# Moving loads, weight splits and a softplus in an attention-and-MLP kernel

## The chip, the cores and the metric

The kernel runs on one core of a Trainium2 chip. The time is the device time of one execution in microseconds (us); lower is better.

## The reference

```python
kv  = einsum('bhsd,bhse->bhde', k, v)          # b, h, s, d = 8, 8, 576, 64
out = einsum('bhsd,bhde->bhse', q, kv)
x   = out / sqrt(mean(out*out, -1) + 1e-6) * g_norm   # laid out as 4608 tokens x 512
h   = x @ w_in                                  # 512 x 2048
g   = h * erf(softplus(h))
y   = g @ w_out                                 # 2048 x 512
```

Everything is float32 (the weights come as float64 and are converted on the chip). Most products are done in a faster float32 form of TensorE (FP32R in the code), for which each operand is split into an upper form, a lower form and a combination of both; three products of these forms replace one exact product. In the trace of the kernel before, the same piece of `h` took 2.7 us in this form (264.02 to 266.74) and 3.4 us exact (146.09 to 149.53).

## The kernel before

The tokens go in nine blocks of 512. Blocks 0 and 1 take the weights as they arrive. While block 1 runs, in sixteen steps, the kernel also splits every weight column block into its three parts and stores the parts (786 KB each) to memory. From the third block on, parts are fetched back in a stream, in periods of four steps. This document calls block 1 "the second block" and what follows "the streamed blocks". Beside this, the attention of the next block is done a piece at a time.

In the profiles PE is TensorE (matmuls), ACT is ScalarE, DVE is VectorE, and SP issues most transfers. Results of TensorE land in banks of the PSUM memory; a bank can be written again when ScalarE or VectorE has copied it out. The copies named below are the *bank copy* (`h_sb`, ScalarE), the *qT copy* (the transposed q, ScalarE) and `bd_kv` (the k-v products, VectorE); the *squares' halves* (`sq_hi`, `sq_lo`) are VectorE's split of the attention's squares.

The loads of k, v and q of one head pair, two pairs ahead:

```python
    def load_pair(i):
        T, p = divmod(i, NP)
        ...
        t = q_sb[T, p] = pool.tile([P, J, 2, D], FP32, name="q_sb", tag="q")
        nc.sync.dma_start(out=t, in_=q[...].rearrange("h (p j) d -> p j h d", j=J))
        for name, got, src in (("k", k_sb, k), ("v", v_sb, v)):
            C = chunks(T)                       # 6 in block 0, else 5
            rows, rest = divmod(S, C)           # 96 and 0, else 115 and 1
            t = got[T, p] = pool.tile([rows + rest, 2, C, D], FP32, ...)
            side.dma_start(out=t[:rows]..., in_=heads[:, : S - rest]...)
            if rest:
                side.dma_start(out=t[rows:, :, 0], in_=heads[:, S - rest :]...)
```

The split of a weight block. The upper form is made by ScalarE in one step, the other two by VectorE at the start of the next, and then the store is issued. `w_new` has four buffers, so a step's uppers need the stores of two steps before to have landed:

```python
    def upper_w(x, high):
        nc.scalar.activation(high, x, AF.Copy, scale=(1.0 + 2.0**-13) / SHIFT)

    def lower_w(x, high, low, both):
        nc.vector.scalar_tensor_tensor(out=low, in0=high, scalar=SHIFT, in1=x, ...)
        nc.vector.tensor_tensor(out=both, in0=high, in1=low, op=ALU.subtract)
```

One step of blocks 0 and 1 (cuts marked with `...`):

```python
    for n in range(FIRST * FC + 1):
        T, f = divmod(n, FC)
        ...
            for key in list(w_new)[:2]:
                w_lower(*key)
            for piece in steps[f][0]:           # halves, norm, split of the attention
                piece()
        ...
            n_ps, m_ps = hidden(T, f, turns=False)
        ...
                nc.scalar.activation(h, n_ps, AF.Copy, scale=SHIFT - 1.0)
                add(h, m_ps)                    # VectorE
            nc.scalar.activation(s, h, AF.Softplus)
            if T == FIRST - 1:
                ...
                gates(done)
                for key in list(w_new):
                    w_lower(*key)
                for key in to_cut[f]:
                    w_upper(*key)
            for piece in steps[f][1]:           # apply, mean
                piece()
            if f % BATCH == BATCH - 1:
                ...                             # four erfs, with two table loads
        if n >= LAG:
            project(f2, hs[n - LAG], last)
        ...
            for piece in steps[f][2]:           # k, v products and q transposes
                piece()
```

And the end of a streamed period, where parts are fetched and finished results are stored:

```python
        for j in range(J):
            result(T2, b2, j, g, w)
            fetch(BATCH + j)                    # the last one fetches two w_out parts
            if b2 == NB - 1:
                store(T2, j, es.pop(j))
```

At the boundary from the second block to the streamed ones, the result tile of block 1 and a tile `h` that the second streamed period fills share a buffer: `h` waits until the last of four result stores has landed.

Of the kernel before, what the change touches and what calls it, by code (L numbers as in the profile page):

```python
# [43 lines left out]
AF = mybir.ActivationFunctionType  # L44
# [11 lines left out]
WHOLE = 2  # L56
# [4 lines left out]
def kernel(  # L61
# [10 lines left out]
    nc = tc.nc  # L72
    P = 128
    B, H, S, D = q.shape
# [6 lines left out]
    FC = DF // P  # L81
# [180 lines left out]

    xT, x_forms, tails = {}, {}, {}

    def attention(T, p, pools=None):

        st = {}

        halves = FIRST <= T < B
# [14 lines left out]
        def products():  # L284

            kv_ps = st["kv"] = bank("kv_ps")
            ks, vs, qs = (x.pop((T, p)) for x in (k_sb, v_sb, q_sb))
            C = chunks(T)
            for c in range(C):
                rows = slice(0, S // C + (c < S % C))  # L290
                for i in range(2):
                    s = slice(i * D, i * D + D)
                    nc.tensor.matmul(  # L293
                        kv_ps[s, s],
                        lhsT=ks[rows, i, c],
                        rhs=vs[rows, i, c],
                        start=(c == 0),
                        stop=(c == C - 1),
                    )
            if p % 2 == 0:  # L300
                nc.tensor.transpose(kv_ps[:, q_tail], q_last[:, p // 2], ident)
            if p == NP - 2:
                for i in range(NP):
                    load_last(T + 1, i)
            st["qT"] = square_tile("qT")
            for i in range(2):
                s = slice(i * D, i * D + D)
                nc.vector.tensor_copy(out=bd[s, s], in_=kv_ps[s, s])
            if p % 2 == 0:
                tails[T] = attp.tile([P, P], FP32, name="qT_last", tag="t")  # L310
                nc.vector.tensor_copy(out=tails[T], in_=kv_ps[:, q_tail])
            st["tail"] = tails[T][:, p % 2 * R : p % 2 * R + R]
            qt_ps = bank("qt_ps")
            for j in range(J):
                nc.tensor.transpose(qt_ps[:, j * P : j * P + P], qs[:, j], ident)  # L315
            nc.scalar.copy(st["qT"], qt_ps)
# [67 lines left out]
            if T >= FIRST:  # L384
                thirds(st.pop("x"), *(form[:, p] for form in x_forms[T]))

        def products_and_loads():
            products()
            load_pair(T * NP + p + 2)

        if T == 0:
            return products, apply, halve, mean, norm
        first = (products_and_loads, apply) if T < B else (lambda: None, square)
        return (*first, halve if halves else lambda: None, mean, norm, split)


    def upper(x, high):
# [163 lines left out]
    first = [attention(0, p, banks_0 | {"se_ps": (ps_o, f"o{p}")}) for p in range(NP)]  # L561
# [51 lines left out]

    others = [("in", f) for f in range(WHOLE)]
    others += [("out", f) for f in (*range(FC - BATCH, FC), *range(FC - BATCH))]
    places_w = {4: 0, 5: 1, 8: 0, 9: 1, FC - 4: 0, FC - 3: 1}
    to_cut = {f: [] for f in range(FC)}
    for f in range(FC):
        if f < FC - BATCH:
            to_cut[f] = [("in", f + WHOLE), others.pop(0)]  # L620
        elif f == FC - BATCH:
            to_cut[f] = [("in", FC - 2), ("in", FC - 1)]
        if f in places_w:
            to_cut[f].append((*others.pop(0), places_w[f]))
# [13 lines left out]
    for n in range(FIRST * FC + 1):  # L638
        T, f = divmod(n, FC)
        if n == FC:  # L640
            early_room.close()
            late = ctx.enter_context(tc.tile_pool(name="late", bufs=1))
            x_new = ctx.enter_context(tc.tile_pool(name="x_new", bufs=1))
            acc = ctx.enter_context(tc.tile_pool(name="acc", bufs=1))
            w_in_p = ctx.enter_context(tc.tile_pool(name="w_in_p", bufs=BATCH))
            low = low_room.enter_context(tc.tile_pool(name="low", bufs=1))
            forms = late.tile([P, 3, KC, G], FP32R, name="x_forms0")
            x_forms[FIRST] = [forms[:, i] for i in range(3)]
        if T < FIRST:
            if f == 0:  # L650
                steps = pieces_of(T + 1)
            if due(1):
                weights()
            for key in list(w_new)[:2]:
                w_lower(*key)
            for piece in steps[f][0]:
                piece()
        while due(0):
            weights()
        done = n - LAG + 1  # L660
        if T == 0 and done >= 0:
            gates(done)
        if T == FIRST - 1:
            if f == 0:
                x_high = wide.tile([P, KC, G], FP32R, name="x_high", tag="h")
                x_low = low.tile([P, KC, G], FP32R, name="x_low")
                for i in range(0, KC, 2):
                    upper(xT[T][:, i : i + 2], x_high[:, i : i + 2])
                for i in range(0, KC, 2):
                    lower_only(xT[T][:, i : i + 2], x_high[:, i : i + 2], x_low[:, i : i + 2])  # L670
        if T == FIRST - 1 and f >= WHOLE:
            n_ps, m_ps = hidden(T, f, turns=False)
        elif T < FIRST:

            if n > 1:
                plain[n] = ps_h.tile([P, G], FP32, name="h_ps", tag="h")
                blocks = [(n, c) for c in range(KC)]
            elif n == 0:
                for i, (pool, tag) in enumerate(((ps_at, "at"), (ps_o, "o0"))):
                    plain[i] = pool.tile([P, G], FP32, name="h_ps", tag=tag)  # L680
                blocks = [(i, c) for c in range(KC - 1) for i in range(2)] + [(0, KC - 1)]
            else:
                blocks = [(1, KC - 1)]
            for i, c in blocks:
                nc.tensor.matmul(  # L685
                    plain[i],
                    lhsT=w_in_sb[:, c, i % FC * P : i % FC * P + P],
                    rhs=xT[T][:, c, :],
                    start=(c == 0),
                    stop=(c == KC - 1),  # L690
                )
        if T < FIRST:
            if n == whole:
                old_h = acc.tile([P, BATCH, G], FP32, name="h", tag="e")
            h = hs[n] = old_h[:, n - whole] if n >= whole else unit("h_sb")
            s = ss[n] = unit("s_sb")
            if n in plain:
                nc.scalar.copy(h, plain.pop(n))
            else:
                nc.scalar.activation(h, n_ps, AF.Copy, scale=SHIFT - 1.0)  # L700
                add(h, m_ps)
            nc.scalar.activation(s, h, AF.Softplus)
            if T == FIRST - 1:
                if f == 1:
                    x_both = wide.tile([P, KC, G], FP32R, name="x_both", tag="h")
                    for i in range(0, KC, 2):
                        both_only(x_high[:, i : i + 2], x_low[:, i : i + 2], x_both[:, i : i + 2])
                    x_forms[T] = x_high, x_low, x_both
                gates(done)
                for key in list(w_new):  # L710
                    w_lower(*key)
                for key in to_cut[f]:
                    w_upper(*key)
            if n == 0:
                w_next("split")
            for piece in steps[f][1]:
                piece()
            if f % BATCH == BATCH - 1:
                for i in range(n - BATCH + 1, n + 1):
                    nc.scalar.activation(ss[i], ss[i], AF.Erf)  # L720
                softplus_table()
            if T == FIRST - 1:
                load_parts("in", {FC - 3: 2, FC - 2: 1, FC - 1: 1}.get(f, 0))
        if n >= LAG:
            T2, f2 = divmod(n - LAG, FC)
            last = n - LAG in (FC - 1, whole - 1)
            project(f2, hs[n - LAG], last)
            if last:
                sums(*((acc, "e") if T2 < FIRST - 1 else (wide, "h")))
                if T2 == 0:  # L730
                    for j in range(J):
                        store(T2, j, es.pop(j))
        if T < FIRST:
            for piece in steps[f][2]:
                piece()
# [44 lines left out]
    for m in range(first_batch, batches + 1):  # L780
        T, b = divmod(m, NB)
# [8 lines left out]
        def piece():  # L790
            if todo:
                todo.pop(0)()
# [22 lines left out]
        if m < batches:  # L815
            h = wide.tile([P, BATCH, G], FP32, name="h", tag="h")
            s = gate_r.tile([P, BATCH, G], FP32, name="s", tag="s")
# [70 lines left out]
```

## Time and profile before

| before | |
|---|---|
| median of the first runs | 960.7 us |
| span of the profiled execution | 958.2 us |
| TensorE busy | 931.0 us, 97% |
| TensorE idle in the second block | 4.15 us, in six waits |
| wait of TensorE at the boundary | 4.10 us |

The page gives the busy time of each engine and, in 40 slices, its busy tenths. The waits say who waited for whom; the timeline shows each instruction with the idle time before it in brackets; the chain of waits goes back from an instruction to what released it. The prediction shows the lines that carry it. One line more of ScalarE's timeline belongs to them (start, us, source line, operation, idle before it and what ended it):

```profile
189.89 0.63 ACT L423 ACTIVATE w_new<-w_in_sb 128x512 fp32r<-128x512 f32 x1 [2.26 <-DMA w_in<-w_new]
191.69 0.64 ACT L423 ACTIVATE w_new<-w_out_sb 128x512 fp32r<-128x512 f32 x1 [1.16 <-DMA w_out<-w_new]
```

At these two lines ScalarE stands still for 3.4 us in all, because two stores have not landed.

### The profile page before, as it was taken

What the parts mean: (1) busy time and instruction counts of PE and PEld (TensorE: products, weight loads), DVE (VectorE), ACT (ScalarE), POOL (GpSimd) and SP (SyncE); (2) the same over time, 40 slices, a digit from 0 to 9 for tenths busy, and PEclk for the clock granted to TensorE, in tenths of its full rate; (3) what the DMA queues carried; (4) which work ended last, traced back from release to release, by engine and by line L of the source; (5) the groups of instructions that cost most, each with busy time, mean ns of one, the idle gap of its engine ahead of it and who ended that gap; (6) DMA issues with size and microseconds to landing.
All of it is one profiled execution on the core that took longest, in us unless ns stands there. A gap on an engine that the chain in (4) does not pass through costs nothing.

```text
span 958.2 us, 11752 instructions
## 1 busy us (share of the span) xinstructions
PE 931.0 (97%) x4272; PEld 684.5 (71%) x4272; DVE 741.0 (77%) x1054; ACT 616.5 (64%) x825; POOL 2.4 (0%) x10
## 2 busy tenths in 40 slices
PE   6999999989998999999999999999999999999998
PEld 4444445556576788888888888888888788878886
DVE  3979957777675788888888888878788877778667
ACT  3889875577663666666666666666666666665552
POOL 0000000000000000000000000000000000000000
PEclk9999999999999999999999999999999999999999
DMA  9857505688899887899888978988897779768872
GB/s 257 284 163 212 159 1 234 253 315 292 287 326 328 322 301 262 249 319 335 305 255 318 331 286 281 317 321 287 271 340 263 263 249 353 274 257 298 337 274 66
DMA packets 111842, 259.78 MB, mean 271 GB/s; under 512 B 43864, under 2 KB 69544, under 8 KB 111784
## 3 DMA queue, kind: packets, MB, share of 16 engines
q1 hardware_dynamic: 110152, 256.73, 76.4%
q10 hardware_dynamic: 1568, 2.29, 0.8%
q8 instruction: 34, 0.56, 0.2%
q14 instruction: 24, 0.20, 0.1%
q0 software_dynamic: 64, 0.00, 0.0%
HBM read 224.40 MB, written 34.60 MB: 270 GB/s over the span
## 4 chain that ended last, share of the span: by engine, by line
PE 78%; ACT 8%; DVE 8%; DMA 4%; issue 1%; SPq 0%; DVEq 0%; ACTq 0%
PE n_ps L456 41%; PE m_ps L456 21%; PE o_ps L514 5%; PE h_ps L685 3%; PE se_ps L321 2%; PE kv_ps L293 2%; PE qt_ps L315 1%; DMA v_sb<-in_v_dram 1%; DMA out_dram<-e 1%; DMA w_out<-w_new 1%; ACT L103 1%; DVE h L848 1%; ACT w_e L215 1%; ACT s_sb L720 1%; DVE h L439 1%
## 5 line engine op out<-in xcount | busy, mean ns | idle before, releaser
L456 PE MATMUL n_ps<-x_forms,w_in_parts 128*128 128x512 f32 x896 | 234.7, 404 | 5.7 <-ACT h L828 4.1
L456 PE MATMUL n_ps<-w_out_parts,g_forms 128*128 128x512 f32 x928 | 231.5, 391 | 0.0
L456 PEld LDWEIGHTS n_ps<-x_forms,w_in_parts 128*128 128x128 f32 x896 | 167.3, 189 | 50.1 <-issue 9.1
L456 PEld LDWEIGHTS n_ps<-w_out_parts,g_forms 128*128 128x128 f32 x928 | 174.1, 188 | 38.7 <-issue 1.7
L830 ACT ACTIVATE s<-h 128x512 f32<-128x512 f32 x112 | 71.0, 634 | 180.4 <-DVE h L439 180.4
L439 DVE TENSOR_TENSOR h<-m_ps,h 128x512 f32<-128x512 f32 x116 | 79.8, 688 | 65.6 <-ACT h L828 50.7
L456 PE MATMUL m_ps<-w_out_parts,g_forms 128*128 128x512 f32 x464 | 124.2, 389 | 0.0
L456 PE MATMUL m_ps<-x_forms,w_in_parts 128*128 128x512 f32 x448 | 120.3, 390 | 0.0
L514 PE MATMUL o_ps<-w_out_sb,h_sb 128*128 128x512 f32 x224 | 100.8, 592 | 0.3 <-DVE h_sb L636 0.3
L456 PEld LDWEIGHTS m_ps<-w_out_parts,g_forms 128*128 128x128 f32 x464 | 87.1, 188 | 18.1
L456 PEld LDWEIGHTS m_ps<-x_forms,w_in_parts 128*128 128x128 f32 x448 | 84.5, 189 | 17.9
L439 DVE TENSOR_TENSOR e<-m_ps,e 128x512 f32<-128x512 f32 x116 | 80.3, 692 | 17.6 <-PE m_ps L456 10.5
L434 DVE SCALAR_TENSOR_TENSOR e<-n_ps,e 128x512 f32<-128x512 f32 x88 | 60.3, 686 | 38.0 <-PE n_ps L456 38.0
L514 PEld LDWEIGHTS o_ps<-w_out_sb,h_sb 128*128 128x128 f32 x224 | 42.3, 190 | 48.9 <-issue 46.6
L828 ACT ACTIVATE h<-n_ps 128x512 f32<-128x512 f32 x112 | 65.6, 586 | 14.1 <-DMA out_dram<-e 10.2
L405 DVE SCALAR_TENSOR_TENSOR g_forms<-g_forms 128x1024 fp32r<-128x1024 f32 x58 | 71.1, 1226 | 2.0
L402 DVE TENSOR_TENSOR g_forms<-h,g_forms 128x1024 fp32r<-128x1024 f32 x58 | 70.6, 1218 | 1.7 <-ACT g_forms L399 1.4
L399 ACT ACTIVATE g_forms<-h 128x1024 fp32r<-128x1024 f32 x58 | 58.9, 1060 | 12.5 <-PE m_ps L456 9.8
L848 DVE TENSOR_TENSOR h<-h,s 128x1024 f32<-128x1024 f32 x56 | 66.0, 1219 | 0.7 <-ACT s L834 0.7
L685 PE MATMUL h_ps<-xT,w_in_sb 128*128 128x512 f32 x144 | 64.9, 594 | 0.8 <-DVE w_in_sb L240 0.6
L106 ACT ACT_TABLE_LOAD x44 | 56.5, 1283 | 0.7
L834 ACT ACTIVATE s<-s 128x1024 f32<-128x1024 f32 x56 | 56.2, 1052 | 0.3
(98 smaller groups left out, 1014.9 us busy)
## 6 DMA issues: line engine op xcount, KB each, us to landing
w_out_parts<-w_out SPq DMA_DIRECT2D x116, 768.0 KB
w_in_parts<-w_in SPq DMA_DIRECT2D x112, 768.0 KB
w_in<-w_new SPq DMA_DIRECT2D x16, 768.0 KB
q_sb<-in_q_dram SPq DMA_DIRECT2D x32, 256.0 KB
w_raw<-in_moe_w_out_dram SPq DMA_DIRECT2D x8, 1024.0 KB
out_dram<-e SPq DMA_DIRECT2D x32, 256.0 KB
k_sb<-in_k_dram SPq DMA_DIRECT2D x28, 287.5 KB
v_sb<-in_v_dram SPq DMA_DIRECT2D x28, 287.5 KB
```

Of the source, the lines that this page charges most:

```text
L106: nc.scalar.preload_act_table_set("softplus")
L399: nc.scalar.activation(high, x, AF.Copy, scale=1.0 + 2.0**-13)
L402: nc.vector.tensor_tensor(out=low, in0=x, in1=high.bitcast(FP32), op=ALU.subtract)
L405: nc.vector.scalar_tensor_tensor(out=both, in0=low.bitcast(FP32), scalar=SHIFT, in1=high.bitcast(FP32), op0=ALU.mult, op1=ALU.add,)
L434: nc.vector.scalar_tensor_tensor(out=out_, in0=ps, scalar=scale, in1=out_, op0=ALU.mult, op1=ALU.add)
L439: nc.vector.tensor_tensor(out=out_, in0=ps, in1=out_, op=ALU.add)
L456: nc.tensor.matmul(ps, lhsT=weights(form, k), rhs=moving(form, k), start=(form == forms[0] and k == 0), stop=(form == forms[-1] and k == 3),)
L514: nc.tensor.matmul(o_ps[j], lhsT=g[:, j * P : j * P + P], rhs=w_out_sb[:, f, :], start=(f == 0), stop=last,)
L685: nc.tensor.matmul(plain[i], lhsT=w_in_sb[:, c, i % FC * P : i % FC * P + P], rhs=xT[T][:, c, :], start=(c == 0), stop=(c == KC - 1),)
L828: nc.scalar.activation(h[:, i], n_ps, AF.Copy, scale=SHIFT - 1.0)
L830: nc.scalar.activation(s[:, i], h[:, i], AF.Softplus)
L848: nc.vector.tensor_tensor(out=part(h, half), in0=part(h, half), in1=part(s, half), op=ALU.mult)
```

## The change

The intent is to let the weight parts through first, to spread the stores, and to use ScalarE's wait for VectorE. Three parts, called A, B and C below. A, the loads:

```diff
-        def products_and_loads():
-            products()
+        def loads():
             load_pair(T * NP + p + 2)
 ...
-        first = (products_and_loads, apply) if T < B else (lambda: None, square)
-        return (*first, halve if halves else lambda: None, mean, norm, split)
+        if T == B:
+            return lambda: None, square, lambda: None, mean, norm, split
+
+        pieces = ((products,), (apply,), (halve, loads)) if halves else ((products, loads), (apply,), ())
+        return (*(partial(chain, *group) for group in pieces), mean, norm, split)
```

B, the list of splits, with w_out ahead of w_in and the six extras elsewhere:

```diff
-    places_w = {4: 0, 5: 1, 8: 0, 9: 1, FC - 4: 0, FC - 3: 1}
+    places_w = {3: 0, 5: 1, 6: 0, 8: 1, 9: 2, 10: 0}
 ...
-            to_cut[f] = [("in", f + WHOLE), others.pop(0)]
+            to_cut[f] = [others.pop(0), ("in", f + WHOLE)]
```

C, the uppers ahead of the softplus:

```diff
-            nc.scalar.activation(s, h, AF.Softplus)
             if T == FIRST - 1:
 ...
                 for key in to_cut[f]:
                     w_upper(*key)
+            nc.scalar.activation(s, h, AF.Softplus)
```

More of the change, by code (lines that the diff above doesn't have):

```diff
@@ L263, with chain @@
     xT, x_forms, tails = {}, {}, {}
+    def chain(*pieces):
+        for piece in pieces:
+            piece()
     def attention(T, p, pools=None):
```

## The prediction

> **What bounds the kernel now.** I read the page's busy shares first, then the waits of TensorE, then its timeline at each wait, then what the waits lead back to. The page:
>
> ```profile
> span 958.2 us, 11752 instructions
> PE 931.0 (97%) x4272; PEld 684.5 (71%) x4272; DVE 741.0 (77%) x1054; ACT 616.5 (64%) x825; POOL 2.4 (0%) x10
> PE   6999999989998999999999999999999999999998
> PEclk9999999999999999999999999999999999999999
> ```
>
> TensorE is busy for 931.0 of 958.2 us, so all its idle time is 27.2 us, 2.8% of the span. The change leaves TensorE's own instructions and their order alone (the comparison of the two kernels' instruction orders has no difference on TensorE; only ScalarE, VectorE and the DMA queue are reordered). It can win only idle time, and what a slowed clock costs after it. The stretch table says where: 2.3 us idle in 20 to 40 us, 1.8 in 60 to 100 (both before anything that the change moves), 4.2 in 160 to 260, 4.6 in 280 to 320, 1.6 in 760 to 860, the rest at the start and at the end. From 320 to 760 TensorE is never idle. So I ask what it waits for in 140 to 320 us (columns: us in total, times, longest):
>
> ```profile
> PE n_ps L456 <- ACT h L828: 4.1, 1, 4.1
> PE se_ps L321 <- ACT qT L316: 2.0, 2, 1.0
> PE n_ps L456 <- ACT h_sb L700: 1.7, 2, 1.0
> ```
>
> The last two, with 0.46 of small ones, are the second token block (148 to 262 us), where the weights are split into parts and stored: idle of 1.02 at 178, 0.20 at 186, 1.03 at 197, 0.65 at 206, 0.99 at 210 and 0.26 at 256 us, 4.15 in all. In the chain of waits, the piece at 197 leads back like this (start, us, what):
>
> ```profile
> 182.68 8.98 DMA w_out<-w_new
> ...
> 191.69 0.64 ACT w_new L423
> ...
> 192.34 1.28 ACT L103
> ...
> 196.96 0.61 ACT h_sb L700
> ...
> 197.61 2.13 PE n_ps L456 x8
> ```
>
> A store of finished parts takes 8.98 us to land, ScalarE waits for its buffer, then does the norm with two table loads, and copies a PSUM bank out too late. The first wait is the boundary to the streamed blocks, here in stretches of 4 us (PE, PEld, DVE, ACT, POOL busy, clock, DMA share, GB/s):
>
> ```profile
> 292.00:296.00 4.00, 3.62 (x14) 2.30 (x13) 0.00 (x0) 0.00 (x0) 0.00 (x0) 1.00 1.02 389
> 296.00:300.00 4.00, 0.29 (x1) 0.29 (x2) 0.30 (x1) 0.60 (x1) 0.00 (x0) 1.00 0.39 128
> 300.00:304.00 4.00, 4.00 (x12) 3.09 (x12) 3.48 (x5) 1.70 (x4) 0.00 (x0) 0.57 1.02 266
> ```
>
> All engines stand; the chain puts 9.86 us here on the last store of a result (issued at 289.06), whose tile the next h needs. After it the clock is 0.57 for 4 us: 4 x 0.43 = 1.7 us more are lost. The boundary costs 4.1 + 1.7 = 5.8 us.
>
> **What the Trainium skill says.** "DMA: Bandwidth & Descriptors", section "Why a DMA increments its semaphore by 16 and not by 1": a copy from these queues runs on k engines, the largest k up to 16 that divides both sides' slowest dimension, the lowest-numbered ones. k and v come as 115 rows: k = 5. The trace agrees: in 296 to 300 us, where only the queue's remainder runs, the share is 0.39, near 5/16 = 0.31, and in 260 to 264 it is 0.32. So k and v put their bytes on five engines, and everything queued behind them completes only when those five have caught up; this is why moving them is more than moving 0.83 MB of 8. The same page, "Queues, rings and completion order", has each engine consume its ring in order, which agrees with a 256 KB store taking 9.86 us behind a backlog. "TensorE: Matmul & The Clock Gate", section "What's actually happening": an idle window of about 3.4 us halves the clock for about as long; the trace shows 0.57 for 4 us after the 4.1 us wait and 1.00 after every shorter one.
>
> **The change, part by part.** Nothing is added or removed: the same 32 weight splits, loads and stores.
>
> *Uppers ahead of the softplus, in the second block.* In each of its 16 steps ScalarE copies a bank, waits for VectorE's add (12.6 + 5.9 us in 14 waits, some 1.3 us each), does the softplus, then 2 or 3 uppers, 0.52 us apart. Now the uppers fill the wait: what follows them comes some 1.0 to 1.3 us earlier, at no cost to VectorE. At 210 us the qT copy came at 209.81 behind three uppers; 1.3 earlier covers the 0.99 us wait: **saved 0.99**. At 178 the qT copy comes early too, but see next.
>
> *Extra splits of w_out moved* from steps 4, 5, 8, 9, 12, 13 to 3, 5, 6, 8, 9, 10. Step 4 loses one: the upper leaves ScalarE, but its lower (two VectorE operations, 0.61 to 0.69 apart, 1.3 us) now runs in step 4 ahead of the result copies and of bd_kv, which ended at 177.08 for a matmul at 177.30. bd_kv goes to about 178.0, a wait of 0.7 where 1.02 was; the squares' halves behind it then come at about 186.1, which TensorE, earlier itself by 0.3, waits 0.3 longer for. Of 1.02 + 0.20, **saved 0.2**.
>
> *k, v and q behind.* In the second block the loads leave step 4p for step 4p + 2. The store with 8.98 us was issued just behind the loads of 179.05 to 182.1 us. Their five-engine share is 115 x 2 x 1280 B x 2 = 589 KB over 5 = 118 KB an engine, 2.4 times the 49 KB that a 786 KB part puts there: with parts at about 2.0 us each, some 5 us, with q 6. Now that store has only the previous extra and the results' stores ahead and lands in about 6 us, near 186, when ScalarE wants the buffer at 185.7 instead of 189.7. The waits of 2.26 and 1.16 us on ScalarE go to about 1, the norm runs some 3 us earlier, the bank is free, and with it the next one at 206: **saved 1.03 + 0.65 = 1.68**. The pairs are used two periods later, so loads that are 10 us later arrive in time.
>
> In the streamed blocks the loads come after the second w_in part of a period. The queue no longer blocks on the k, v, q buffers (it waited 59.8 us for the transposes there), but from 320 to 760 TensorE waits for no transfer: **0**. At the boundary, 12 parts, one k, v, q set and three stores stand in the queue ahead of the last store, before and after alike. On the five engines that is 12 x 2.0 + 6 + 4 stores x 0.7 + latency 1.2 = 34 us or more from 263 us, to 297 or later (landed: 298.9). The start is set by the four w_out parts, issued when the last gates of the block are done, which stays tied to TensorE. So the boundary moves with the rest: **saved 0**, at best a few tenths.
>
> Sum: 0.99 + 0.2 + 1.68 = 2.9, with a few tenths at the boundary 3.2 us: 960.7 - 3.2 = **957.5 us**.
>
> **Rivals.** (1) *The uppers become a wait.* They stand before the softplus now and need a buffer whose store was issued a step before; with 3 parts in steps 8, 9 and 10 and the loads behind step 5's and 9's stores, the five engines get 13.7 parts' worth (27 us) in a group of steps of 28 us. ScalarE could stall 2 to 5 us at steps 8, 9 and 12. For it: the share was already 0.94 to 1.06 in 184 to 200 and 212 to 228. Against: TensorE has two pieces of slack there. If so, the gain is eaten: 959 to 962. (2) *The boundary wait goes.* If the end of the second block is freed of its last two extra stores and the parts start earlier, the last store needs to land 4.8 us sooner relative to TensorE; then 5.8 us go as well: about 951. Against: the engines were almost idle at 260 to 263 already (share 0.03 and 0.06 in single microseconds), so there was no backlog to free. If only the clock dip goes (a wait just short enough), it is 955 to 956. (3) *All is hidden*: VectorE is busy 11.7 of 12 us in 176 to 188 and again in 208 to 220, and sets the pace there whatever ScalarE does; then the gain is about 1 us: 959.7.
>
> **Range and chances.** The whole of what can be won is 4.15 + 5.8 + 0.45 = 10.4 us, 1.1%: faster by over 2% is not in reach. A loss of 2%, 19 us, would need a new wait in every streamed period, where loads still have more than one period in hand. I put the low end at 953.5, between the clock dip going and the boundary wait going, and the high end at 960.5, where rival 1 or 3 eats nearly all. Chances 0.01, 0.985, 0.005.
>
> **What would show it.** In the changed kernel's waits of TensorE, the two on ACT qT and the two on ACT h_sb should be gone or under 0.3 us, and a wait on DVE bd_kv or sq_lo of 0.5 to 1 us in all should stand in the second block; its idle time should be 1 to 1.5 us instead of 4.15. No store of w_out should take 9 us ahead of the norm in step 6. The boundary should still show a wait of about 4 us on ACT h, ended by the out store, and a clock near 0.57 after it. From there to the end TensorE's instructions should take as long as before. The prediction is wrong if the boundary wait shrinks by over 1.5 us, if a wait for a parts transfer or a k, v load appears on TensorE, or if ScalarE's uppers wait longer than 3 us and a bank copy behind them comes late.

## The result and the profile after

The changed kernel took 953.82 us (953.3 to 954.02, 4 runs) against 960.35 us (959.8 to 961.76, 4 runs). The ratio is 0.9929, with a 95% interval of 0.9912 to 0.9946. A ratio here is the mean time of one kernel's fast runs over that of the other's of the same rounds, so not quite the ratio of the medians quoted. That is 0.7% faster, within 2%, and inside the predicted range, near its low end: about 6.5 us were gained where 3.2 were forecast.

The page of the changed kernel, and what its TensorE waited for in 140 to 320 us:

```profile
span 952.2 us, 11746 instructions
PE 929.1 (98%) x4272; PEld 684.7 (72%) x4272; DVE 740.4 (78%) x1054; ACT 616.1 (65%) x825; POOL 2.4 (0%) x10
```

```profile
PE n_ps L462 <- ACT h L834: 3.4, 1, 3.4
PE qt_ps L319 <- DVE x L378: 0.5, 1, 0.5
PE o_ps L520 <- DVE h_sb L642: 0.3, 1, 0.3
```

All waits on the qT copy and on the bank copies (`h_sb`) are gone from the second block; one of 0.3 us is left of six. The boundary wait is still there. Its stretches of 4 us (PE, PEld, DVE, ACT, POOL busy, clock, DMA share, GB/s) and the chain behind it:

```profile
288.00:292.00 4.00, 2.45 (x11) 1.69 (x9) 0.00 (x0) 0.00 (x0) 0.00 (x0) 1.00 1.02 420
292.00:296.00 4.00, 2.14 (x5) 1.72 (x6) 2.12 (x3) 1.71 (x3) 0.00 (x0) 0.75 0.80 291
296.00:300.00 4.00, 4.00 (x16) 3.21 (x15) 2.46 (x5) 1.68 (x4) 0.00 (x0) 0.82 0.67 194
```

```profile
283.21 9.85 DMA out_dram<-e
...
293.21 0.61 ACT h L834
```

The last result store still takes 9.85 us, the wait after it is 3.4 instead of 4.1 us, and the clock loses 4 x 0.25 + 4 x 0.18 = 1.7 us, as before.

Three landmarks of TensorE's timeline, here before and after, divide the difference of the spans, 6.0 us.

```profile
153.64 0.80 PE L456 MATMUL n_ps<-x_high,w_new 128*128 128x512 f32 x1
256.28 3.70 PE L514 MATMUL o_ps<-w_out_sb,h_sb 128*128 128x512 f32 x8 [0.26 <-DVE h_sb L636]
317.24 0.66 PE L315 MATMUL qt_ps<-ident,q_sb 128*128 128x128 f32 x4 [0.45 <-DVE x L374]
```

```profile
154.22 0.80 PE L462 MATMUL n_ps<-x_high,w_new 128*128 128x512 f32 x1
251.30 3.70 PE L520 MATMUL o_ps<-w_out_sb,h_sb 128*128 128x512 f32 x8 [0.30 <-DVE h_sb L642]
311.39 0.66 PE L319 MATMUL qt_ps<-ident,q_sb 128*128 128x128 f32 x4 [0.45 <-DVE x L378]
```

The first fast product of the second block came at 153.64 before and 154.22 after, although nothing ahead of it was changed: 0.6 us lost in the start. From there to the end of the block's last projection it was 106.34 and 100.78 us: **5.6 us gained**. From there to the q transposes of the third streamed period it was 57.26 and 56.39 us: **0.9 us gained**. The rest is equal to 0.1 us; from 320 to 760 us TensorE was busy 440.00 and 439.87 of 440 us.

### The profile page after: what moved, and what is told of

Its sections match the earlier page's. It is cut to its first block, busy times and chain, and to the rows that moved or that the text cites. A ratio compares the mean times of both kernels' runs of the same rounds, so it can differ in the third digit from the quotient of the medians.

```text
span 952.2 us, 11746 instructions
## 1 busy us (share of the span) xinstructions
PE 929.1 (98%) x4272; PEld 684.7 (72%) x4272; DVE 740.4 (78%) x1054; ACT 616.1 (65%) x825; POOL 2.4 (0%) x10
## 4 chain that ended last, share of the span: by engine, by line
PE 83%; ACT 6%; DVE 6%; DMA 3%; SPq 1%; issue 1%; DVEq 0%; ACTq 0%
PE n_ps L462 42%; PE m_ps L462 21%; PE o_ps L520 8%; PE h_ps L691 3%; PE se_ps L325 3%; PE kv_ps L297 2%; PE qt_ps L319 2%; DMA out_dram<-e 1%; DMA w_in_parts<-w_in 1%; SPq L136 1%; ACT w_e L215 1%; ACT L103 1%; DVE h L445 1%; ACT w_m L219 1%; DMA q_sb<-in_q_dram 1%
```

## The experiments

All twelve runs gave correct results. "Block" is the second landmark distance, "idle" the recorded idle time of TensorE in it, "boundary" the wait on ACT h, "from h" the span less the start of the first h matmul. The last is there because the start, whose code is common to all, ended between 27.9 and 30.3 us. These four columns are from the one profiled execution. The ratio is to the kernel before of the same rounds; the runs on chip 10 went in one call, those on chip 6 in two, with a shared set of runs of the kernel before.

| kernel | what | ratio (95%) | block | idle | boundary | from h |
|---|---|---|---|---|---|---|
| before | | 1 | 106.34 | 4.15 | 4.10 | 930.3 |
| after | A + B + C | 0.9929 (0.9912 to 0.9946) | 100.78 | 0.30 | 3.41 | 923.7 |
| e1_loads (chip 10) | A | 0.9966 (0.9953 to 0.9978) | 102.65 | 1.44 | 3.44 | 925.7 |
| e2_cuts (10) | B | 1.0027 (1.0012 to 1.0041) | 108.47 | 6.06 | 3.18 | 932.1 |
| e3_uppers (10) | C | 0.9984 (0.9970 to 0.9998) | 104.97 | 3.23 | 2.27 | 926.8 |
| k112 (10) | A + B + C, 112-row loads | 0.9932 (0.9917 to 0.9946) | 100.76 | 0.30 | 0.41 | 920.8 |
| u1_no_loads (6) | B + C | 1.0024 (1.0005 to 1.0042) | 108.18 | 5.13 | 2.68 | 930.5 |
| u2_no_cuts (6) | A + C | 0.9937 (0.9919 to 0.9955) | 100.80 | 0.30 | 2.56 | 922.8 |
| u3_no_uppers (6) | A + B | 0.9981 (0.9963 to 0.9998) | 104.16 | 2.35 | 3.45 | 927.1 |
| k6 (6) | A + B + C, 96-row loads | 0.9941 (0.9924 to 0.9957) | 100.93 | 0.30 | 0.68 | 923.6 |
| after_again (6) | A + B + C | 0.9941 (0.9921 to 0.9960) | 100.83 | 0.30 | 3.54 | 923.9 |
| s1_store_first (6) | A + B + C, stores ahead | 0.9894 (0.9876 to 0.9912) | 100.77 | 0.30 | none | 919.0 |
| b112 (6) | before, 112-row loads | 0.9955 (0.9937 to 0.9972) | 103.36 | 1.88 | 2.08 | 924.9 |
| s2_store_112 (6) | s1 + 112-row loads | 0.9894 (0.9873 to 0.9914) | 100.76 | 0.30 | none | 919.5 |

My theory going in was the prediction's: A frees the slow store, C frees the qT copies, B does little, and the boundary belongs to the DMA queue. The rival was that one part does it all and the others are decoration.

### One part alone: e1_loads, e2_cuts, e3_uppers

e1_loads is the kernel before with A:

```diff
-        first = (products_and_loads, apply) if T < B else (lambda: None, square)
+        pieces = ((products,), (apply,), (halve, loads)) if halves else ((products, loads), (apply,), ())
```

> The kernel before with only the k, v and q loads moved. Theory (the prediction's): the store that took 8.98 us to land is no longer behind k and v, so the waits of 1.03 and 0.65 us near 197 and 206 us go; those of 1.02 and 0.99 us on the qT copy stay. Idle time of TensorE in the second block 4.15 to about 2.4 us, the run 1.7 to 2.3 us shorter than before. Rival (the uppers' place matters, the loads do not): idle stays near 4 us, gain under 0.7 us. The boundary wait stays 3.4 to 4.1 us in both.

It gained 0.34% (955.93 against 959.45 us). ScalarE no longer waits for any store in the block. The two waits on the bank copies went, as the theory said; but of the two waits on the qT copy one went too, the one at step 9. It had not been a fault of the step's own order: it came from ScalarE still being late from step 6. The bank copy that TensorE waited for at 206 us started 5.79 us after its product in the kernel before and 3.43 us after it here, the next one 2.00 and 0.52 us. The block is 3.7 us shorter, more than the 1.7 to 2.3 us expected.

e2_cuts is the kernel before with B:

```diff
-    places_w = {4: 0, 5: 1, 8: 0, 9: 1, FC - 4: 0, FC - 3: 1}
+    places_w = {3: 0, 5: 1, 6: 0, 8: 1, 9: 2, 10: 0}
```

> The kernel before with only the split list reordered (w_out first, extras in steps 3, 5, 6, 8, 9, 10). Theory: one upper less in step 4 brings the qT copy 0.5 us earlier, of a wait of 1.02; the long store is still behind k and v; gain 0 to 1 us. Rival (VectorE is full and the extra lowers in steps 4 and 6 hurt): 0 to 1 us slower.

It lost 0.27% (961.62 us, 2.2 us by the medians), the rival's sign and over twice its size. The wait that the prediction foresaw for B does exist here, with two others:

```profile
179.36 0.43 PE L320 MATMUL kv_ps<-qT_last,bd_kv 128*128 128x64 f32 x2 [1.46 <-DVE bd_kv L308]
187.17 0.50 PE L342 MATMUL ms_ps<-sq_hi,mean_w 128*128 128x512 f32 x1 [0.24 <-DVE sq_hi L334]
200.23 0.50 PE L456 MATMUL n_ps<-x_high,w_new 128*128 128x512 f32 x1 [2.19 <-ACT h_sb L700]
```

The extra lower of step 3 runs on VectorE ahead of bd_kv, and with the loads unmoved the stores are still late. At the boundary this kernel's clock is slowed for 6.8 us, where it is 3.4 us in the kernel before.

e3_uppers is the kernel before with C:

```diff
-            nc.scalar.activation(s, h, AF.Softplus)
 ...
                     w_upper(*key)
+            nc.scalar.activation(s, h, AF.Softplus)
```

> The kernel before with only the uppers ahead of the softplus. Theory: both waits on the qT copy (1.02, 0.99 us) go, those behind the slow store stay; idle 4.15 to about 2.1 us, gain 2 to 2.7 us. Rival (ScalarE being earlier also hides the slow store): all four waits go, gain 4 to 5.5 us, and the other two parts are worth nothing.

It gained 0.16% (957.37 us); the block gained 1.4 us, less than expected. Both waits on qT went. But the uppers, now first, meet the late stores with more force:

```profile
190.00 0.63 ACT L423 ACTIVATE w_new<-w_in_sb 128x512 fp32r<-128x512 f32 x1 [4.76 <-DMA w_in<-w_new]
191.78 0.63 ACT L423 ACTIVATE w_new<-w_out_sb 128x512 fp32r<-128x512 f32 x1 [1.15 <-DMA w_out<-w_new]
```

4.76 us where it was 2.26: ScalarE starts to wait earlier, and the softplus now waits behind it. The bank copy behind the norm is as late as before (1.15 us of wait at 198 us). The larger part of the idle time left is elsewhere, though: TensorE waits for the squares' halves, VectorE's work, 0.67 and 0.23 us at 186 and 0.65 and 0.23 us at 217. This is the prediction's first rival, in a kernel where A does not prevent it.

### One part undone: u1_no_loads, u2_no_cuts, u3_no_uppers

u1_no_loads is the changed kernel without A:

```diff
-        pieces = ((products,), (apply,), (halve, loads)) if halves else ((products, loads), (apply,), ())
+        first = (products_and_loads, apply) if T < B else (lambda: None, square)
```

> The changed kernel with only the loads put back where they were. Theory: the stores of step 4 are again behind k and v, ScalarE waits 2 to 3.5 us for a buffer in step 6, now ahead of the softplus, and the bank copy behind it is late: 1.7 to 2.3 us slower than the changed kernel (about 956). Rival (the other two parts do it all): within 0.5 us of the changed kernel.

It is slower than the kernel before (1.0024), and against the changed kernel on the same chip by 1.0024 / 0.9941 = 1.0083, 8 us. Four times what I expected. ScalarE's timeline shows why:

```profile
193.14 0.63 ACT L427 ACTIVATE w_new<-w_out_sb 128x512 fp32r<-128x512 f32 x1 [5.23 <-DMA w_out<-w_new]
195.04 0.63 ACT L427 ACTIVATE w_new<-w_in_sb 128x512 fp32r<-128x512 f32 x1 [1.27 <-DMA w_in<-w_new]
```

TensorE then waits 3.27 us for a bank at 202 us, and the clock is slowed in the block itself:

```profile
202.00:204.00 2.00, 2.00 (x5) 1.61 (x6) 2.00 (x4) 1.98 (x4) 0.00 (x0) 0.50 0.34 133
```

The slowed stretch lasts from 201.44 to 204.86 us; after the wait, which ends at 201.99, that is 2.9 us at half the clock, by estimate 1.4 of the 8 us. B and C without A are a loss: A is what lets the others pay.

u2_no_cuts is the changed kernel without B:

```diff
-    places_w = {3: 0, 5: 1, 6: 0, 8: 1, 9: 2, 10: 0}
+    places_w = {4: 0, 5: 1, 8: 0, 9: 1, FC - 4: 0, FC - 3: 1}
```

> The changed kernel with only the old split list. Theory: in step 4 the third upper fits into ScalarE's wait and nothing else changes: 0 to 1 us slower. The last stores of steps 12 and 13 then come late and meet the first w_in parts, but TensorE doesn't wait for them. Rival (the moved extras are what frees the end of the block): a wait for w_in parts or 2 us and more slower.

It is equal to the changed kernel (0.9937 and 0.9941, block 100.80 and 100.83 us). As the theory had it, B is worth nothing beside A and C.

u3_no_uppers is the changed kernel without C:

```diff
                     w_upper(*key)
-            nc.scalar.activation(s, h, AF.Softplus)
```

> The changed kernel with the softplus again ahead of the uppers. Theory: the wait of about 1 us at step 9 on the qT copy is back, that at step 5 half back (two uppers instead of three): 1.3 to 2.5 us slower than the changed kernel. Rival (loads and splits alone do it): within 0.5 us.

It is 0.9981 / 0.9941 = 1.0040 of the changed kernel, 3.8 us slower, more than the 1.3 to 2.5 us expected. The wait is not where I said. The qT copy costs 0.15 us; TensorE waits 1.45 us for bd_kv at 180 us, VectorE's queue, and then for both halves of the squares:

```profile
179.68 0.43 PE L324 MATMUL kv_ps<-qT_last,bd_kv 128*128 128x64 f32 x2 [1.45 <-DVE bd_kv L312]
```

So C pays through VectorE too: with the erfs of step 3 earlier, VectorE gets to the x form behind them at 171.81 us in the changed kernel and at 174.11 here (the starts are 0.2 us apart), which makes room for B's extra lower.

### The five engines: k112, b112, k6

k112 is the changed kernel with the 115-row loads cut in two, 112 rows and 3:

```diff
-            side.dma_start(out=t[:rows]..., in_=heads[:, : S - rest]...)
+            whole_rows = rows // 16 * 16
+            parts_of = heads[:, : S - rest].rearrange("h (r c) d -> r h (c d)", c=C)
+            for lo, up in ((0, whole_rows), (whole_rows, rows)):
+                if lo < up:
+                    side.dma_start(out=t[lo:up]..., in_=parts_of[lo:up])
```

> The changed kernel with each k and v load of 115 rows cut into one of 112 rows and one of 3, same bytes to the same places. Theory (115 rows run on 5 of 16 DMA engines, and these five set when the last result store lands at the boundary): 112 rows spread over 16, the store lands 4 to 5 us earlier relative to TensorE, the boundary wait of 3.4 us and the slowed clock after it go: about 5 us faster than the changed kernel, 948 to 950 us. Rival (total bytes in the queue set it): the boundary wait stays over 2.5 us and the run is within 1 us of the changed kernel, or slower by the added issues.

In the profiled execution the boundary wait fell from 3.4 to 0.41 us, as the theory of the five engines says, the clock stayed at full speed, and the execution took 950.49 us. The four timed ones took 952.96 to 953.93 us, so that the ratio, 0.9932, is no better than that of the changed kernel, measured on other chips (0.9929, 0.9941). Why these four lack the gain is open. They have no trace, but the record has their mean clock: 1.000, 0.999, 0.999 and 0.997. A slowed clock of 3.4 us takes 0.002 off the mean, so in three of them the loss is not a slowed boundary. The start differs between profiled executions by up to 2.3 us, which would nearly be enough, but that is an argument and was not shown. The profiled execution also shows that some of the boundary comes back as other waits: TensorE then stands 0.69 and 0.23 us for the halves of the squares near 297 us (0.68 and 0.22 in k6).

b112 is the kernel before with the same cut and nothing else:

```diff
-            side.dma_start(out=t[:rows]..., in_=heads[:, : S - rest]...)
+            for lo, up in ((0, whole_rows), (whole_rows, rows)):
+                side.dma_start(out=t[lo:up]..., in_=parts_of[lo:up])
```

> The kernel before with k and v loads of 112 and 3 rows. Theory (the load move helped because k and v load five engines on which the stores behind them wait): the stores behind the loads land about 4 us earlier without any move, the waits near 197 and 206 us go, and the boundary wait too: 3.5 to 7 us faster than before, with the two waits on the qT copy left. Rival (the order itself, or the blocked queue, was what mattered): waits near 197 and 206 us stay, gain under 1.5 us in the second block.

This is the run that tells the five engines from the order. The order is that of the kernel before, loads ahead of stores, yet the waits on the bank copies went, and what was left of ScalarE's waits for stores is one line:

```profile
190.91 0.63 ACT L426 ACTIVATE w_new<-w_out_sb 128x512 fp32r<-128x512 f32 x1 [0.69 <-DMA w_out<-w_new]
```

0.69 us instead of 2.26 + 1.16. The waits on the qT copy stand at 0.94 and 0.44 us. The block is 3.0 us shorter, against 3.7 us by moving the loads, and the whole is 0.9955. The packet records show the spread itself: from 100 us on, packets of k and v (1280 bytes) were in flight for 150.8 us in the kernel before, 5 to 7 of them at once for 75% of that time and 8 or more for 0.2%; in b112 for 72.4 us, 8 or more at once for 66%. So A helps because loads of 115 rows hold up what is queued behind them; spreading the loads does nearly the same in the block without moving them. The boundary wait shrank to 2.1 us only, which is less than the theory claimed.

k6 takes six chunks of 96 rows everywhere:

```diff
-        return 6 if T == 0 else 5
+        return 6
```

> The changed kernel with k and v in six chunks of 96 rows instead of five of 115 in every block: 96 rows spread over 16 DMA engines, at four more 64 x 64 matmuls for each of 16 pairs, 16 x 4 x 0.037 = 2.4 us on TensorE (worked out from 20 in 0.73 us). Theory of the five engines: boundary wait and slow clock gone (5.1 us), so net 2 to 3 us faster than the changed kernel. Rival (bytes, not engines): boundary wait over 2.5 us, 2 us slower than the changed kernel.

The boundary wait fell to 0.68 us and the clock stayed up, as expected; but the time is that of the changed kernel (0.9941 both), not 2 to 3 us better. Against k112, which has the same spread without the added matmuls, it is 2.8 us longer from the first h matmul to the end. The estimate of 2.4 us had counted 16 pairs; the trace has 112 more matmul records (4384 against 4272), four for each of 28 pairs, which at the estimate's 0.037 us makes 4.1 us. I had reckoned the boundary at more than it turned out to give here.

### What stands ahead of the last store: s1_store_first, s2_store_112, after_again

```diff
             result(T2, b2, j, g, w)
-            fetch(BATCH + j)
             if b2 == NB - 1:
                 store(T2, j, es.pop(j))
+            fetch(BATCH + j)
```

> The changed kernel with each result store issued ahead of the part fetch of its step instead of behind it. Theory (the last result store lands when the DMA engines have worked off what is queued ahead, here two w_out parts of 786 KB less, some 4 us): the boundary wait of 3.4 us falls under 1 us, the slowed clock after it goes, 3 to 5 us faster than the changed kernel. Rival (the store's landing is latency, or k and v on five engines alone): the wait stays over 2 us, and the blocked queue delays the w_out parts: same or slower.

> The changed kernel itself, on the same chip as the three below, as their yardstick: ratio to the kernel before 0.992 to 0.994.

s1_store_first took 949.03 us (948.83 to 950.21) where the changed kernel, on the same chip, took 953.96 (951.82 to 955.12): 0.9894 / 0.9941 = 0.9953, 4.5 us. It beats both kernels. The wait of ScalarE on the store, and the stretches at the boundary:

```profile
ACT h L834 <- DMA out_dram<-e: 4.8, 1, 4.8
```

```profile
288.00:292.00 4.00, 4.00 (x19) 3.30 (x18) 3.15 (x4) 1.72 (x3) 0.00 (x0) 1.00 1.02 422
292.00:296.00 4.00, 3.83 (x18) 2.84 (x16) 2.35 (x5) 2.71 (x5) 0.00 (x0) 1.00 0.80 274
```

ScalarE waits 4.8 instead of 9.5 us, TensorE not at all for it, and the clock stays at 1.00. The last store takes 6.09 us instead of 9.85 and is issued 1.2 us earlier. Two parts fewer ahead of it are worth 4.7 us of ScalarE's wait, near the 4 us of the estimate: the store's time is mostly the backlog ahead of it. From the block's end to the third period's transposes it is 51.67 us instead of 56.39.

s2_store_112 joins both edits, the `fetch` behind the `store` and the cut loads:

```diff
-            fetch(BATCH + j)
             if b2 == NB - 1:
                 store(T2, j, es.pop(j))
+            fetch(BATCH + j)
 ...
+            for lo, up in ((0, whole_rows), (whole_rows, rows)):
```

> Both: stores ahead of the fetches and 112-row loads. Theory: either removes the boundary wait, so both together give no more than the better of the two, within 1.5 us of the one with the stores first. Rival (they add up): over 2 us faster than it.

It is equal to s1 (0.9894 both): two ways to remove one wait do not add up.

## Why the prediction was right, and where its sum was off

**What bounds the kernel, and that only idle time can be won: right.** TensorE's order did not change, and outside the second block and the boundary nothing moved by more than the 0.6 us of the start. But 4.15 us was not all that could be won in the block, as the next points show. That the time still lies in the range is in part luck: the low end, 953.5 us, allowed for a part of the boundary that did not go, and this made room for a block gain that the prediction had held out of reach.

**The boundary stays: right in the main.** Predicted 0 to a few tenths; measured 0.7 us less wait and the same 1.7 us of slowed clock, 0.9 us by the landmarks. In other runs with other orders the wait was anything from 2.1 to 3.5 us; A does not decide it (3.44 with A alone, 2.27 with C alone, 2.68 with B and C). What does, beyond the bytes ahead of the store and their spread, is open. s1 shows that the mechanism named, the backlog, is the one. (The 1.2 us of latency in the prediction's sum for the store rest on no run here.)

**The sum for the second block, 2.9 us: too small; it was 5.6.** Three terms failed. In numbers: the forecast of 2.87, and 1.02 for the waits at 178 and 186 us that were to stay, less 0.04 for the wait at the block's end, and 1.71 us beyond the brackets make 5.56.

- *The term for an idle wait.* The prediction took the recorded idle time as the cost. Removing 4.15 - 0.30 = 3.85 us of recorded idle shortened the block by 5.56 us. It is so in each run: taking the changed kernel as the floor, 1.14 us of idle cost 1.87 us in e1, 2.05 cost 3.38 in u3, 5.76 cost 7.69 in e2. Each wait costs some 0.3 us more than its bracket. The records show where much of it goes: without a wait a record starts before the one ahead of it ends, and the bracket counts from that end only. Here are the same two products of step 4 before and after, 1.35 and 0.17 us apart: 1.18 us for a bracket of 1.02.

```profile
177.30 0.33 PE L320 MATMUL kv_ps<-qT_last,bd_kv 128*128 128x64 f32 x2
178.65 1.12 PE L321 MATMUL se_ps<-qT,bd_kv 128*128 128x512 f32 x2 [1.02 <-ACT qT L316]
```

```profile
177.87 0.33 PE L324 MATMUL kv_ps<-qT_last,bd_kv 128*128 128x64 f32 x2
178.04 1.08 PE L325 MATMUL se_ps<-qT,bd_kv 128*128 128x512 f32 x2
```

- *"Of 1.02 + 0.20, saved 0.2".* All of it went, and 1.66 us with it: from the projection at 16 us into the block to that at 33 us it took 16.98 us before and 15.32 after. The step that failed is "bd_kv goes to about 178.0". VectorE's extra lower does go ahead of bd_kv; but C also brings the erfs of step 3 and the x form behind them forward (its VectorE work began at 171.81 instead of 172.90 us, in a run that was 0.6 us behind in the start), and that pays for the lower. Without C there is a wait on bd_kv, 1.45 us in u3 and 1.46 in e2, twice the 0.7 us predicted with C. So two of the prediction's signs did not come: a wait on bd_kv or sq_lo of 0.5 to 1 us, and an idle time of 1 to 1.5 us, which was 0.30.
- *The shares of the parts.* They do not add: A is worth 3.7 us of the block alone and 7.4 where B and C are in (some 1.4 of it u1's slowed clock); C is worth 1.4 alone and 3.4 where A and B are; B costs 2.1 alone and gives nothing beside the others. The waits near 197, 206 and 210 us were one delay handed from engine to engine, not three faults: A alone removes all three. The prediction assigned the 0.99 us at 210 to C; C alone removes it too (e3), so it was counted for one part where either is enough. The wait near 178 stands apart: it is 1.00 us in e1 and 0.94 in b112, and goes with C.

**The loads on five engines: right**, the step that carried the argument for A. b112 shows it without any move. One of the two readings given for it is wrong, though: the share of 0.32 in 260 to 264 us is the mean of 0.34, 0.03, 0.06 and 0.86 in its four microseconds. The packets in flight (see b112) are the better evidence.

**The first rival, uppers that become a wait: false for this kernel, true for its neighbours.** In the changed kernel ScalarE did wait 1.7 + 1.3 us for stores in the block, and TensorE felt none of it. In e3 and u1 it waited 10.0 and 10.3 us in all (7.6 + 2.4, 3.0 + 7.3). In u1 this and the clock ate the gain; in e3 TensorE lost 1.15 us behind it and 1.8 us for the squares' halves.

**Faster by over 2% not in reach, slower not likely: right.**

## What to carry to other kernels

Before adding up waits, ask which are one delay seen several times: undo parts of a change one by one as well as doing them one by one, because a part can be worth nothing, or harmful, until another has removed what it would run into. A transfer that uses few of the DMA engines delays what is queued behind it by more than its bytes suggest (here the same bytes kept packets in flight for 150.8 or 72.4 us), so choose row counts that spread, or put what is urgent ahead of it. And where a buffer is released by a store, look at what is queued ahead of that store: moving each step's fetch behind its store was worth 4.5 us here, two thirds of the whole change.

## What the Trainium skill lacked or had wrong

- "DMA: Bandwidth & Descriptors", section "Why a DMA increments its semaphore by 16 and not by 1", gives the number of engines rightly (115 rows, 5 engines: 5 to 7 packets of k and v in flight for 75% of their time). No page gives a measured cost for the transfers queued behind such a one: cutting each load into 112 + 3 rows, and nothing else, shortened the block by 3.0 us and the kernel to 0.9955, and took ScalarE's waits for stores from 3.4 to 0.7 us.
- "TensorE: Matmul & The Clock Gate", section "What's actually happening", puts the slowed clock after an idle window of about 3.4 us. Here it came after recorded waits of 2.08 us (b112: 0.72 and 0.50 in the stretches of 2 us after it) and 2.27 us (e3), and did not come after waits of 2.19 us (e2) and 2.68 us (u1). So a wait well under 3.4 us can be enough, and its length alone does not decide it. The clock records of the 14 traces show more: every slowed stretch starts a whole number of periods of 3.413 us after the first entry of its record (81, 82 or 83 periods at the boundary, 53 in u1's block). Cut into these periods (without the last one of each run), the runs were slowed after each of the 15 in which TensorE was busy for at most 39% (39% in b112, 33% in e3), and after none in which it was busy for 46% or more (49% in e2, 50% in u1). So the window need not be idle; where between 39% and 46% the limit lies was not measured.
- No page gives what a short wait of TensorE costs beyond its recorded idle time: some 0.3 us each here, 5.56 us of block for 3.85 us of idle. "Perfetto Trace Analysis", section "Identifying the Most-Contended Engine", warns that matmul busy time does not measure how close a kernel is to its roofline (the limit of the hardware). That agrees: for the same 4272 matmuls TensorE counted as busy for 931.0 us before and 929.1 after.
